# Moving the last modulation rows of a transformer block from TensorE to VectorE and GpSimd

## The chip, the core and the metric

One core of one Trainium2 chip runs the whole kernel. The metric is the device time of one execution in microseconds (us). Its engines work side by side, each through its own queue of instructions in order: TensorE (PE; its weight loads are listed as PEld), VectorE (DVE), ScalarE (ACT), GpSimd (POOL) and SyncE (SP, which here only issues DMAs).

## The reference

Input x is 2048 rows (tokens) of 1024 numbers in bf16. A condition vector c gives six modulation rows of 1024 numbers each; the block is a linear attention and a SwiGLU MLP, each behind a modulated layernorm:

```python
mod = (_silu(c) @ w_mod).reshape(c.shape[0], 6, 1, -1)
sa, ca, ga, sb, cb, gb = (mod[:, i] for i in range(6))
h = _layernorm(x) * (1 + ca) + sa
x = x + ga * linear_attention(h, wqkv, wo)     # 32 heads of 32, phi(t) = elu-like, denominator per token
h = _layernorm(x) * (1 + cb) + sb
x = x + gb * ((silu(h @ w_gate) * (h @ w_up)) @ w_down)    # hidden width 3584
```

Each row is a product of one vector of 1024 numbers with a 1024x1024 slice of w_mod (2 MB in bf16). This case is about three of them: ga (index 2), sb (3) and cb (4).

## The kernel before

**Stages.** A prologue computes silu(c), the rows sa and ca (on TensorE, loads `wme`), the layernorm of the first 512 tokens and the first K groups. Then the tokens go by in four chunks of 512 (`sc` 0 to 3). For each chunk TensorE computes K (`k_phase`, 8 groups), the previous chunk's K^T V product (`kv_phase`), and V (`v_phase`, 8 groups); a group is 8 matmuls of 128x128 by 128x512 into one accumulator. Chunk 0 also does its Q groups. After the chunks come the remaining Q groups, mixed with the folding of wo (`fold_wo`), then the attention output of chunk 0 (`wo_tile`, four tiles of 128 tokens), and then per chunk the MLP (`gate_up`, `down`), with the next chunk's `wo_tile`s inside `down`.

**Evacuation.** A K or Q group's accumulator is emptied by `phi_to`: an exp on ScalarE (L289), then two VectorE instructions (L290, L292), the last of which frees the accumulator. A V group is emptied by a ScalarE copy (L327). The accumulators of these groups (`acc_a`) rotate over four PSUM banks.

**The layernorm of the next chunk.** While chunk `sc` runs, `ln1(sc+1)` works on the next: for each of four tiles of 128 tokens, VectorE takes the BN statistics (L218, L219, `veps` L210), GpSimd raises to the power -1/2 (`rstd`, L212) and forms `nmr` (L226), ScalarE normalises to `xn` (L228), and SyncE issues a DMA that transposes `xn` into `hT` (L256). When all four have landed, VectorE scales and shifts `hT` block by block (`modulate_all`, L231, 8 instructions). The next chunk's first K group reads that `hT`. The same steps, for the second layernorm, follow each `wo_tile` (L607 to L617).

**The rows ga, sb, cb before.** `mod_load` brings 1 MB blocks of w_mod (`wml`) over SyncE's queue: two for ga in chunk 1, four for sb and cb in chunk 2. TensorE contracts them with silu(c), which was copied 32 times over columns (`sc32`), in the middle of the K phase of chunks 2 (`ga_rows`) and 3 (`mod_rows`), 32 matmuls each. ScalarE copies the result out, and GpSimd issues small DMAs that write it to DRAM and read it back: ga broadcast over the 128 partitions, sb and cb as columns (`mcol`). `ga_bc` multiplies the weights wo (L553). The row gb is done differently already: VectorE multiplies the 1024-wide row blocks with silu(c), one number per partition (`gb_sum`, L366 and L368), adding eight of them in `gb_acc`, and GpSimd sums over the 128 partitions and broadcasts (`partition_all_reduce`, L703).

**Order.** A scheduler in the framework places the instructions on each engine; `tc.issue_after(x)` gives what follows in the text no place before instruction x, and TensorE keeps the order of the text. Big buffers (`big`, 19 of 8 KB per partition) come free when their last reader is done; x1 tiles are three, ScalarE's and VectorE's scratch `e` and `eb` three each.

Of the kernel before, what the change touches and what calls it, by code (L numbers as in the profile page):

```python
# [9 lines left out]
ALU = mybir.AluOpType  # L10
# [11 lines left out]
def kernel(  # L22
# [13 lines left out]
    nc = tc.nc  # L36
# [72 lines left out]
    def acc_b(name, shape=(NB,), dt=F32):  # L109
        return pb.tile([P] + list(shape), dt, name=name, tag="pb")  # L110
# [193 lines left out]
    def k_evac(sc, gs, accs):  # L304
        for (t, nb), acc in zip(gs, accs):
            phi_to(pks[sc][:, t, nb * NB:(nb + 1) * NB], acc[:])

    def k_phase(sc, lo, hi):
        if lo == 0:
            pks[sc] = big("pk", [STC, D])  # L310
        for g in k_groups[lo:hi]:
            accs = [acc_a()]
            k_mms(sc, [g], accs)
            k_evac(sc, [g], accs)

    def v_phase(sc):
        v = big("v", [VT + DH])
# [8 lines left out]
                                     start=(cc == 0), stop=(cc == DC - 1))  # L326
                nc.scalar.copy(out=v[:, t * D + nb * NB:t * D + (nb + 1) * NB], in_=acc[:])  # L327

    def q_phase(sc, lo=0, hi=DC):
        if lo == 0:  # L330
            pqs[sc] = big("pq", [HG, SCW])
        for qc in range(lo, hi):
            acc = acc_a()
            for cc in range(DC):
                mm(acc[:], lhsT=wq[cc // 4][:, cc % 4, qc * P:(qc + 1) * P], rhs=hTs[sc][:, cc, :],
                                 start=(cc == 0), stop=(cc == DC - 1))
            phi_to(pqs[sc][:, qc, :], acc[:])

    def v_ones(v, lo):
        head = v[:, lo:lo + DH]  # L340
# [26 lines left out]
            else:  # L367
                nc.vector.scalar_tensor_tensor(out=gb_acc[:], in0=t[:], scalar=sc, in1=gb_acc[:], op0=ALU.mult, op1=ALU.add)  # L368

    def ga_rows(blks):  # L370
        ps = acc_b("modr")
        H2 = NB // 2
        for j in range(DC):
            for g in range(4):
                mm(ps[32 * g:32 * g + 32, 0:H2], lhsT=sc32[:, j, :], rhs=blks[g // 2][:, j, (g % 2) * H2:(g % 2 + 1) * H2],
                   start=(j == 0), stop=(j == DC - 1))
        row = small.tile([P, NB], BF16, name="mrow", bufs=1)
        nc.scalar.copy(out=row[:, 0:H2], in_=ps[:, 0:H2])
        for g in range(4):
            nc.gpsimd.dma_start(out=mrow_dram[0, g:g + 1, 0:H2], in_=row[32 * g:32 * g + 1, 0:H2])  # L380
        nc.gpsimd.dma_start(out=ga_bc.rearrange("p (g n) -> p g n", g=4),
                            in_=mrow_dram[0, :, 0:H2].unsqueeze(0).to_broadcast([P, 4, H2]))

    gb_rows = []

    def mod_load(cols):
        blks = []
        for lo in cols:
            t = big("wml", [DC, NB])
            nc.sync.dma_start(out=t[:], in_=wm_v[:, :, lo:lo + NB])  # L390
            blks.append(t)
        return blks

    def mod_rows(blks):
        ps = acc_b("modr")
        for j in range(DC):
            for g in range(4):
                mm(ps[32 * g:32 * g + 32, :], lhsT=sc32[:, j, :], rhs=blks[g][:, j, :],
                                 start=(j == 0), stop=(j == DC - 1))
        row = small.tile([P, NB], BF16, name="mrow", bufs=1)  # L400
        nc.scalar.copy(out=row[:], in_=ps[:])
        return row

    mrow_dram = dram.tile([2, 4, NB], BF16, name="mrow_scratch")

    def mod_spread(k, row):
        for g in range(4):
            nc.gpsimd.dma_start(out=mrow_dram[k, g:g + 1, :], in_=row[32 * g:32 * g + 1, :])
        cols = small.tile([P, 2 * DC], BF16, name="mcol", bufs=1)
        with nc.allow_non_contiguous_dma(reason="2048 elements, once"):  # L410
            nc.gpsimd.dma_start(out=cols[:], in_=mrow_dram[1].rearrange("g (i p) -> p (g i)", p=P))
        nc.vector.tensor_copy(out=sbT[:], in_=cols[:, 0:DC])
        nc.vector.tensor_scalar_add(out=cb1T[:], in0=cols[:, DC:2 * DC], scalar1=1.0)

    def modulate_all(hT, scaleT, biasT):
        for cc in range(DC):
# [21 lines left out]
    def den_spread(sc):  # L438
        rb = rbs.pop(sc)
        for q in range(STC):  # L440
            nc.gpsimd.dma_start(out=rden_dram[sc, :, q * P:(q + 1) * P], in_=rb[32 * q:32 * q + 32, :])
        rbc = big("rbc", [HG, SCW])
        rv = rden_dram[sc].rearrange("(h g) t -> h (g t)", h=HPC)
        for h in range(HPC):
            nc.gpsimd.dma_start(out=rbc[h * DH:(h + 1) * DH].rearrange("p g t -> p (g t)"),
                                in_=rv[h].unsqueeze(0).to_broadcast([DH, HG * SCW]))
        rbcs[sc] = rbc

    def den_apply(sc):
        pq, rbc = pqs[sc], rbcs.pop(sc)  # L450
# [6 lines left out]
    def keep_warm(acc, n):  # L457
        for _ in range(n):
            mm(acc[:], lhsT=sel[:, 0, :], rhs=sel[:], start=True, stop=True)

    gs = k_groups[0:6]
    accs = [acc_a() if i < 4 else acc_b("acc") for i in range(6)]
    spare = accs[5]
    keep_warm(spare, 9)
    hT = hTs[0] = big("hT", [DC, SCW])
    pks[0] = big("pk", [STC, D])
    H = 3 * P
    with in_order(nc.vector, nc.scalar, nc.gpsimd):
# [36 lines left out]
        k_mms(0, gs7, accs7, 0, A)  # L505
        for cc in range(A, DC):
            modulate(hT, cc, ca1T, saT)
        k_mms(0, gs + gs7, accs + accs7, A, DC)
        gs8, accs8 = k_groups[7:8], [acc_b("acc")]
        k_mms(0, gs8, accs8)  # L510
        k_evac(0, gs, accs)
        k_evac(0, gs7, accs7)
        k_evac(0, gs8, accs8)
    with tc.issue_after(last_on[nc.gpsimd.engine]):
        build_masks()
        nc.gpsimd.tensor_copy(out=scf[:], in_=scT[:])

    for sc in range(NSC):
# [39 lines left out]
    nc.vector.tensor_tensor(out=Zden[:], in0=kv_acc[:, :, DH:DH + 1].to_broadcast([P, HG, DH]),  # L558
# [141 lines left out]

    def gb_last():
        gb_sum(5, DC)
        nc.gpsimd.partition_all_reduce(gb_bc[:], gb_acc[:], P, bass_isa.ReduceOp.add)  # L703
# [45 lines left out]
```

## Time and profile before

| | |
|---|---|
| time, median of 3 runs | 836.31 us (836.17 to 836.62) |
| the profiled execution: its own time | 836.56 us |
| its span in the trace | 834.7 us |
| instructions | 11272 |
| DMA | 129.07 MB |

The profile is one profiled execution. Times in it are counted from the start of the span. "Busy" is the time in which an engine had an instruction at work; a group of instructions is named by line, engine, operation and what it writes and reads. The chain that ended last is followed back from the last instruction, at each step to what released it. A DMA issue has two times, that of the issue on its queue and that from issue to landing. A line of an order or a timeline may hold several like instructions ("x8"). TensorE's granted clock in that execution was 1.00 in every stage looked at.

### The profile page before, as it was taken

The numbers are of one execution on the slowest core, as the hardware profiler recorded it, in microseconds if no ns is written. First come the engines' busy times: TensorE is split into PE (matmuls) and PEld (weight loads), VectorE is DVE, ScalarE is ACT, GpSimd is POOL, SyncE is SP. The second block draws the span as 40 slices with busy tenths as digits, with TensorE's granted clock in tenths as the row PEclk, the third lists the DMA queues.
The fourth block names the chain that finished last, engine by engine and source line by source line (L and its number), as shares of the span: only waits on it lengthen the run. The fifth ranks groups of instructions, "written<-read, shape, count | busy, mean of one in ns | idle before, by whom it ended". The sixth has DMA issues, their size and how long they took to land.

```text
span 834.7 us, 11272 instructions
## 1 busy us (share of the span) xinstructions
PE 828.2 (99%) x4641; PEld 378.6 (45%) x4641; DVE 317.6 (38%) x606; ACT 168.6 (20%) x253; POOL 67.5 (8%) x168
## 2 busy tenths in 40 slices
PE   8999999999999999999999999999999999999998
PEld 3444444444444444444444444444444444444444
DVE  5755643587344335522222244211114431111122
ACT  3455443334211111101111110111110101111000
POOL 2101201111130201100000010000001100000000
PEclk9999999999999999999999999999999999999999
DMA  9873790129998644636434183662505529710011
GB/s 325 293 202 88 227 194 1 34 61 290 359 247 265 190 151 144 185 117 219 144 114 138 44 227 95 220 221 82 171 1 155 162 69 332 239 53 1 19 58 51
DMA packets 125748, 129.07 MB, mean 155 GB/s; under 512 B 34112, under 2 KB 106304, under 8 KB 125184
## 3 DMA queue, kind: packets, MB, share of 16 engines
q1 hardware_dynamic: 121440, 114.97, 45.7%
q0 software_dynamic: 3968, 12.99, 5.4%
q8 instruction: 36, 0.59, 0.3%
q10 hardware_dynamic: 288, 0.40, 0.1%
q14 instruction: 16, 0.13, 0.1%
HBM read 108.27 MB, written 12.72 MB: 145 GB/s over the span
## 4 chain that ended last, share of the span: by engine, by line
PE 95%; DMA 3%; SPq 1%; DVE 0%; issue 0%; ACT 0%
PE acc L98 88%; PE a_ps L98 7%; DMA wv<-in_A_wqkv_dram 1%; DMA x_sb<-in_A_x_dram 1%; DMA wme<-in_w_mod_dram 1%; PE kvp L98 1%; SPq L140 0%; PE modr L98 0%; PE den L98 0%; SPq L120 0%; DVE wo L577 0%; PE wf L98 0%; SPq L137 0%; DVE pq L292 0%; ACT eb L289 0%
## 5 line engine op out<-in xcount | busy, mean ns | idle before, releaser
L98 PE MATMUL acc<-h2T,wgu 128*128 128x512 bf16 x1792 | 387.6, 379 | 0.0
L98 PEld LDWEIGHTS <-wgu 128*128 128x128 bf16 x1792 | 175.3, 98 | 211.3
L98 PE MATMUL acc<-wd,gu 128*128 128x512 bf16 (+2 forms) x924 | 196.1, 373 | 0.0
L646 DVE TENSOR_TENSOR gu<-acc,e 128x512 bf16<-128x512 f32 x112 | 77.5, 692 | 289.9 <-PE acc L98 289.9
L645 ACT ACTIVATE e<-acc 128x512 f32<-128x512 f32 x112 | 66.9, 597 | 374.8 <-PE acc L98 374.8
L98 PEld LDWEIGHTS <-gu 128*128 128x128 bf16 x924 | 89.3, 98 | 104.5
L98 PEld LDWEIGHTS <-hT 128*128 128x128 bf16 x512 | 49.6, 98 | 60.0 <-issue 1.4
L667 DVE TENSOR_TENSOR e<-acc,gb_bc 128x512 f32<-128x512 f32 (+2 forms) x33 | 22.3, 675 | 131.5 <-PE acc L98 128.6
L98 PE MATMUL a_ps<-wo,pq 128*128 128x512 bf16 x256 | 57.4, 379 | 0.0
L98 PE MATMUL acc<-wk,hT 128*128 128x512 bf16 x256 | 57.1, 379 | 0.0
L98 PE MATMUL acc<-hT,wq 128*128 128x512 bf16 x256 | 56.8, 379 | 0.0
L98 PE MATMUL acc<-wv,hT 128*128 128x512 bf16 x256 | 56.1, 379 | 0.3 <-DMA wv<-in_A_wqkv_dram 0.3
L289 ACT ACTIVATE eb<-acc 128x512 bf16<-128x512 f32 x64 | 37.8, 596 | 74.1 <-PE acc L98 71.0
L228 ACT ACTIVATE xn<-x,nmr,rstd 128x1024 bf16<-128x1024 f32 x16 | 19.8, 1240 | 126.2 <-POOL nmr L226 126.2
L614 POOL DMA_DIRECT2D x_scratch<-x x16 | 9.9, 616 | 377.3 <-DVE x L607 377.3
L98 PEld LDWEIGHTS <-pq 128*128 128x128 bf16 x256 | 25.1, 98 | 30.2
L98 PEld LDWEIGHTS <-wq 128*128 128x128 bf16 x256 | 24.6, 98 | 29.8 <-issue 0.9
L290 DVE TENSOR_SCALAR eb<-eb 128x512 bf16<-128x512 bf16 x64 | 18.5, 294 | 49.4 <-ACT eb L289 49.3
L607 DVE TENSOR_TENSOR x<-a_ps,x_sb 128x512 f32<-128x512 f32 x32 | 22.1, 691 | 7.8 <-PE a_ps L98 7.7
L212 POOL TENSOR_TENSOR rstd<-veps,neg_half 128x1 f32<-128x1 f32 x32 | 17.9, 560 | 80.9 <-DVE veps L210 70.8
L327 ACT CAST v<-acc 128x512 bf16<-128x512 f32 x32 | 18.2, 582 | 23.2 <-PE acc L98 23.2
L670 DVE TENSOR_TENSOR ob<-e,x1r 128x512 bf16<-128x512 f32 (+2 forms) x33 | 22.3, 676 | 1.0
(82 smaller groups left out, 274.6 us busy)
## 6 DMA issues: line engine op xcount, KB each, us to landing
wgu<-in_B_w_gate_dram SPq DMA_DIRECT2D x28, 1024.0 KB, 7.3
wgu<-in_B_w_up_dram SPq DMA_DIRECT2D x28, 1024.0 KB, 8.8
x_sb<-in_A_x_dram SPq DMA_DIRECT2D x32, 256.0 KB, 7.2
x_scratch<-x POOLq DMA_DIRECT2D x16, 512.0 KB, 3.1
x1r<-x_scratch SPq DMA_DIRECT2D x31, 256.0 KB, 2.8
wd<-in_B_w_down_dram SPq DMA_DIRECT2D x7, 1024.0 KB, 7.3
wml<-in_w_mod_dram SPq DMA_DIRECT2D x6, 1024.0 KB, 9.0
rbc<-rden_scratch POOLq DMA_DIRECT2D x16, 256.0 KB, 9.3
```

What stands on the lines that cost most here:

```text
L98: return tc.keep_in_program_order(nc.tensor.matmul(out, lhsT=lhsT, rhs=rhs, start=start, stop=stop))
L212: nc.gpsimd.tensor_tensor(out=rstd[:, 0:n], in0=veps[:, 0:n], in1=neg_half[:].to_broadcast([P, n]), op=ALU.pow)
L228: nc.scalar.activation(out=dst, in_=src, func=ACT.Identity, bias=nmr[:], scale=rstd[:, 0:1])
L289: nc.scalar.activation(out=e[:], in_=acc, func=ACT.Exp)
L290: nc.vector.tensor_scalar(out=e[:], in0=e[:], scalar1=1.0, scalar2=PHI_EPS, op0=ALU.min, op1=ALU.add)
L327: nc.scalar.copy(out=v[:, t * D + nb * NB:t * D + (nb + 1) * NB], in_=acc[:])
L607: nc.vector.tensor_tensor(out=x1[:, ns], in0=a_ps[:], in1=x_t[:, ns], op=ALU.add)
L614: nc.gpsimd.dma_start(out=x1_dram[st * P:(st + 1) * P, :], in_=x1[:])
L645: nc.scalar.activation(out=sg[:], in_=ps[0][:], func=ACT.Silu)
L646: gm = nc.vector.tensor_tensor(out=guT[sc][f // GPT][:, f % GPT, :], in0=ps[1][:], in1=sg[:], op=ALU.mult)
L667: nc.vector.tensor_tensor(out=yt, in0=y_ps, in1=gb_bc[:, ns], op=ALU.mult)
L670: nc.vector.tensor_tensor(out=ob, in0=yt, in1=x1r, op=ALU.add)
```

## The change

For ga, sb and cb, the contraction goes the way that gb's goes already, in halves of 512 columns. `mod_begin(q)` takes an x1 tile as accumulator and loads two 1 MB blocks; `mod_step(n)` issues the next n of the 48 VectorE instructions (16 per row), each multiplying a 128x512 block by one number per partition and adding it. Their numbers per place are written out: two after each of Q groups 3 and 4 of chunk 0, `K_STEPS` of them one by one in the K phase of chunks 1 to 3 (4, 6, 8), `V_STEPS` in the V phase (6, 6, 12), two in Q group 0 of chunk 1. GpSimd sums over partitions (`mod_total`): ga in chunk 2 straight into `ga_bc`, sb in chunk 3, cb behind `den_spread(0)`; sb and cb go through DRAM in one row DMA each and come back as columns. The loads of row 2, 3 and 4 are moved to chunk 0, 1 and 2. wo x ga moves from the end of chunk 2 to the V phase of chunk 3, the copy of sb and cb into their places to behind Q group 7 of chunk 2. In the prologue, zeros matmuls that keep TensorE busy are partly issued as fp32 with half the columns of bf16's number: 4 + 1 for 9, and 3 for 6.

```diff
@@ k_phase
             k_mms(sc, [g], accs)
             k_evac(sc, [g], accs)
+            mod_step(int(k_groups.index(g) < K_STEPS[sc]))
@@
-    def q_phase(sc, lo=0, hi=DC):
+    def q_phase(sc, lo=0, hi=DC, steps=0):
...
             phi_to(pqs[sc][:, qc, :], acc[:])
+            mod_step(steps)
@@
-    def ga_rows(blks):
...
-    def mod_load(cols):
...
-    def mod_rows(blks):
...
-    def mod_spread(k, row):
...
+    mrow_dram = dram.tile([2, D], BF16, name="mrow_scratch")
+    mod_steps = []
+
+    def mod_begin(q):
+        acc = x1p.tile([P, D], F32, name="x1")
+        for half in range(2):
             t = big("wml", [DC, NB])
+            nc.sync.dma_start(out=t[:], in_=wm_v[:, :, q * D + half * NB:q * D + (half + 1) * NB])
+            mod_steps.extend((acc[:, half * NB:(half + 1) * NB], t, j) for j in range(DC))
+        return acc
+
+    def mod_step(n):
+        if n == 0:
+            return
+        with tc.issue_after(last_phi[0].ins):
+            for _ in range(n):
+                acc, t, j = mod_steps.pop(0)
+                if j == 0:
+                    nc.vector.tensor_scalar(out=acc, in0=t[:, 0, :], scalar1=scf[:, 0:1], scalar2=None, op0=ALU.mult)
+                else:
+                    nc.vector.scalar_tensor_tensor(out=acc, in0=t[:, j, :], scalar=scf[:, j:j + 1], in1=acc,
+                                                   op0=ALU.mult, op1=ALU.add)
+
+    K_STEPS = [0, 4, 6, 8]
+    V_STEPS = [0, 6, 6, 12]
+
+    def mod_total(dst, acc):
+        nc.gpsimd.partition_all_reduce(dst, acc[:], P, bass_isa.ReduceOp.add)
+
+    def mod_row(k, acc):
+        row_t = ep.tile([P, NB], F32, name="e")
+        row = row_t[:].bitcast(BF16)
+        mod_total(row, acc)
+        nc.gpsimd.dma_start(out=mrow_dram[k:k + 1, :], in_=row[0:1, :])
+
+    def mod_cols():
         cols = small.tile([P, 2 * DC], BF16, name="mcol", bufs=1)
...
+            nc.gpsimd.dma_start(out=cols[:], in_=mrow_dram[:].rearrange("k (i p) -> p (k i)", p=P))
+        return cols
@@
+    def keep_warm_f32(acc, n):
+        zeros = sel[:].rearrange("p h n -> p (h n)").bitcast(F32)
+        for _ in range(n):
+            mm(acc[:, 0:zeros.shape[1]], lhsT=zeros[:, 0:P], rhs=zeros, start=True, stop=True)
@@
-    keep_warm(spare, 9)
+    keep_warm_f32(spare, 4)
+    keep_warm(spare, 1)
@@
-        keep_warm(spare, 6)
+        keep_warm_f32(spare, 3)
@@ the loop over chunks
             k_phase(sc, 2, 4)
             if sc == 2:
-                ga_rows(blks)
-            if sc == 3:
-                mod_spread(1, mod_rows(blks))
+                mod_total(ga_bc, rows[2])
             k_phase(sc, 4, 8)
-            if sc == 1:
-                blks = mod_load([2 * D, 2 * D + NB])
-            if sc == 2:
-                blks = mod_load([3 * D, 3 * D + NB, 4 * D, 4 * D + NB])
+        if sc == 0:
+            rows[2] = mod_begin(2)
         v_phase(sc)
...
         if sc == 0:
-            q_phase(0, 0, 6)
+            q_phase(0, 0, 3)
+            q_phase(0, 3, 5, 2)
+            q_phase(0, 5, 6)
+        elif sc + 1 < NSC:
+            rows[sc + 2] = mod_begin(sc + 2)
+        else:
+            mod_row(0, rows[3])
+        if sc + 1 == NSC:
+            with tc.issue_after(last_phi[0].ins):
+                for cc in range(DC):
+                    w = wo[cc // 4][:, cc % 4, :]
+                    nc.vector.tensor_tensor(out=w, in0=w, in1=ga_bc, op=ALU.mult)
+        mod_step(V_STEPS[sc])
...
-            for cc in range(DC):
-                w = wo[cc // 4][:, cc % 4, :]
-                nc.vector.tensor_tensor(out=w, in0=w, in1=ga_bc, op=ALU.mult)
-
-    q_phase(1, 0, 2)
+
+    q_phase(1, 0, 1, 2)
+    q_phase(1, 1, 2)
@@
-    den_spread(0)
+    spread = den_spread(0)
+    with tc.issue_after(spread.ins):
+        mod_row(1, rows[4])
+        cols = mod_cols()
@@ behind q_phase(2, 6, 8)
+    with tc.issue_after(last_phi[0].ins):
+        nc.vector.tensor_copy(out=sbT[:], in_=cols[:, 0:DC])
+        nc.vector.tensor_scalar_add(out=cb1T[:], in0=cols[:, DC:2 * DC], scalar1=1.0)
```

On the built program's queues the change stands so, as far as the prediction speaks of it. GpSimd: after the rstd and nmr of chunk 1 comes an instruction that changes its loaded code, then the sum for ga, a change back, and only then the four rstd and nmr of `ln1(3)`; another change and the sum for sb in chunk 3; the sum for cb behind the DMAs of `den_spread(0)`, and the change back behind the first DMA of `wo_tile(0)`. SyncE: the 1 MB `wml` loads of rows 3 and 4 stand between the transposes of `hT` for chunks 2 and 3, the second half of each directly ahead of the fourth transpose. ScalarE: in chunk 2 each of the four normalisations stands ahead of a V copy, the first ahead of the first.

More of the change, by code (lines that the diff above doesn't have):

```diff
@@ L368, in gb_sum @@
                 nc.vector.scalar_tensor_tensor(out=gb_acc[:], in0=t[:], scalar=sc, in1=gb_acc[:], op0=ALU.mult, op1=ALU.add)
-    def ga_rows(blks):
[L371 to L382, printed above, removed]
@@ L384 @@
-    gb_rows = []
-    def mod_load(cols):
-        blks = []
-        for lo in cols:
-            t = big("wml", [DC, NB])
-            nc.sync.dma_start(out=t[:], in_=wm_v[:, :, lo:lo + NB])
-            blks.append(t)
-        return blks
-    def mod_rows(blks):
[L395 to L402, printed above, removed]
@@ L404 @@
-    mrow_dram = dram.tile([2, 4, NB], BF16, name="mrow_scratch")
-    def mod_spread(k, row):
-        for g in range(4):
-            nc.gpsimd.dma_start(out=mrow_dram[k, g:g + 1, :], in_=row[32 * g:32 * g + 1, :])
+    gb_rows = []
+    mrow_dram = dram.tile([2, D], BF16, name="mrow_scratch")
[3 more added lines that the diff above has]
+        for half in range(2):
+            t = big("wml", [DC, NB])
+            nc.sync.dma_start(out=t[:], in_=wm_v[:, :, q * D + half * NB:q * D + (half + 1) * NB])
+            mod_steps.extend((acc[:, half * NB:(half + 1) * NB], t, j) for j in range(DC))
+        return acc
@@ L409, in mod_spread @@
+    K_STEPS = [0, 4, 6, 8]
[8 more added lines that the diff above has]
+    def mod_cols():
         cols = small.tile([P, 2 * DC], BF16, name="mcol", bufs=1)
         with nc.allow_non_contiguous_dma(reason="2048 elements, once"):
-            nc.gpsimd.dma_start(out=cols[:], in_=mrow_dram[1].rearrange("g (i p) -> p (g i)", p=P))
@@ L412, in mod_spread @@
-        nc.vector.tensor_copy(out=sbT[:], in_=cols[:, 0:DC])
-        nc.vector.tensor_scalar_add(out=cb1T[:], in0=cols[:, DC:2 * DC], scalar1=1.0)
+            nc.gpsimd.dma_start(out=cols[:], in_=mrow_dram[:].rearrange("k (i p) -> p (k i)", p=P))
+        return cols
     def modulate_all(hT, scaleT, biasT):
@@ L444, in den_spread @@
         for h in range(HPC):
-            nc.gpsimd.dma_start(out=rbc[h * DH:(h + 1) * DH].rearrange("p g t -> p (g t)"),
-                                in_=rv[h].unsqueeze(0).to_broadcast([DH, HG * SCW]))
+            last = nc.gpsimd.dma_start(out=rbc[h * DH:(h + 1) * DH].rearrange("p g t -> p (g t)"),
+                                       in_=rv[h].unsqueeze(0).to_broadcast([DH, HG * SCW]))
         rbcs[sc] = rbc
+        return last
     def den_apply(sc):
@@ L516 @@
         nc.gpsimd.tensor_copy(out=scf[:], in_=scT[:])
+    rows = {}
     for sc in range(NSC):
@@ L702, in gb_last @@
         gb_sum(5, DC)
-        nc.gpsimd.partition_all_reduce(gb_bc[:], gb_acc[:], P, bass_isa.ReduceOp.add)
+        mod_total(gb_bc[:], gb_acc)
     gb_acc = x1p.tile([P, D], F32, name="x1")
```

## The prediction

> **What bounds the kernel now.** I read the engine shares first, then the chain that ended last in order of time (start us, us, what).
>
> ```profile
> PE 828.2 (99%) x4641; PEld 378.6 (45%) x4641; DVE 317.6 (38%) x606; ACT 168.6 (20%) x253; POOL 67.5 (8%) x168
> ```
> ```profile
> 20.90 10.64 DMA wv<-in_A_wqkv_dram
> ...
> 91.99 3.56 PE acc L98 x16
> 95.55 0.99 PE modr L98 x32
> 96.54 24.28 PE acc L98 x112
> ...
> 125.53 1.84 PE modr L98 x32
> ```
>
> TensorE sets the end: up to 31.5 us the chain runs through loads, then it is TensorE nearly without a gap. The two `modr` pieces, 0.99 and 1.84 us, are the contractions that the change takes off TensorE. Eight matmuls of one accumulator take 1.73 us (96.54 to 120.82 is 14 of them). So what matters is whether a chunk's `hT` is ready when its first K group wants it. That is read from the rows that scale `hT` on VectorE:
>
> ```profile
> 84.39 2.68 DVE L231 TENSOR_SCALAR hT<-hT,sca 128x512 bf16<-128x512 bf16 x8 [6.52 <-DMA hT<-xn]
> ...
> 111.69 2.67 DVE L231 TENSOR_SCALAR hT<-hT,sca 128x512 bf16<-128x512 bf16 x8 [5.38 <-DMA hT<-xn]
> ```
>
> Both wait for the last transpose by DMA. Chunk 1's V phase ends at 87.3 (63.11 + 14 x 1.73), chunk 2's at 117.3 (96.54 + 12 x 1.73). The scaled `hT` begins 2.9 us before the first and 5.6 us before the second: that is all the slack there is.
>
> **What GpSimd's sum over partitions costs.** The kernel has one already, for gb, on an idle stretch. The timeline of GpSimd:
>
> ```profile
> 269.75 6.13 POOL L703 PARTITION_ALL_REDUCE gb_bc<-x  x1 [23.39 <-DVE x L368]
> ...
> 316.94 0.58 POOL L614 DMA_DIRECT2D x_scratch<-x  x1 [39.48 <-DVE x L607]
> 325.11 0.59 POOL L212 TENSOR_TENSOR rstd<-veps,neg_half 128x1 f32<-128x1 f32 x1 [7.58 <-DVE x L607]
> ```
>
> VectorE's `veps` for that rstd was done at 317.80, yet the power began at 325.11. Between them lies only an instruction that changes GpSimd's loaded code:
>
> ```profile
> L212 POOLq MODIFY_POOL_CONFIG  x2: 37/37/37, 317.6 to 317.6; - x2
> ```
>
> From it to the first power 7.5 us pass. The other change, at 246.4, lay 23 us ahead of its sum and cost nothing. A transpose queued behind a 1 MB load is the second price; queue of SyncE, then issue to landing of that transpose, then of one at 479 us with no load just ahead:
>
> ```profile
> 328.86 0.79 SPq L631 DMA_DIRECT2D wgu<-in_B_w_gate_dram  x1
> 329.74 2.24 SPq L617 DMA_TRANSPOSE h2T<-xn  x1
> ```
> ```profile
> DMA to landing us min/median/max: 6.4/6.4/6.4
> ```
> ```profile
> DMA to landing us min/median/max: 3.2/3.2/3.2
> ```
>
> The load landed 6.3 us after its issue, at 335.2, the transpose at 336.1: 0.9 us after it.
>
> **What the Trainium skill says.** "GPSIMD Engine Reference", 2.1 Instruction dispatch: the first call after code is loaded pays about 6 us with no instruction to show for it; the trace agrees in kind and reads 7.5. "DMA: Bandwidth & Descriptors", Queues, rings and completion order: each DMA engine takes one issuer's descriptors in ring order; the 6.4 against 3.2 us fits. "Advanced Engine Details and Errata", GPSIMD Details: GpSimd conflicts with VectorE instructions in a two-port mode or with two SBUF inputs; no row of before shows it, as the VectorE rows inside the one sum read PSUM and keep 0.69 us. "TensorE: Matmul & The Clock Gate", What's actually happening: an idle window of about 3.4 us halves the clock; before never idles so long.
>
> **The change, part by part.**
>
> Removed: 64 `modr` matmuls, **-2.83 us** on the path. Their two ScalarE copies, eight small row DMAs, the broadcast of ga and its wait lay beside other work: 0.
>
> Added on VectorE: 3 x 16 steps on 128x512, by the 128x1024 rows of gb (1.28 and 0.75 us) and the 0.69 us two-input rows about 0.7 us each (0.5 the first of each half), some 33 us in chunks 0 to 3. Chunk 0: q groups 3 and 4 get two steps each; VectorE has 0.71 us free per group, so it falls 0.7 us late, the scaling of `hT` for chunk 1 starts at 57.3 instead of 56.65, wanted from 58.5: 0. A K group is 0.98 us of phi in 1.73 us; one step fits. Chunk 3: eight steps in K, then wo x ga (eight at 0.62, moved here from chunk 2 and early chunk 3) and eleven steps in V: 13.5 us from 18.7 to 32.2 us after the chunk's start, while the V phase ends at 28.8. What is late next is Zden, at 36.7, wanted at about 36.85: 0, at most +1.
>
> Chunk 1. The steps push the BN rows: the fourth `veps` comes at 79.4 instead of 77.7, so the fourth xn is done at 81.75 and its transpose issues at 81.8 (before: 80.69). The program puts the 1 MB load of the next `wml` just ahead of that transpose on SyncE's queue (issue about 81.2, once the third is issued). Landing: 81.2 + 6.3 + 0.9 = 88.4. The eight scalings start 0.334 us apart, so the eighth ends at 88.5 + 2.75; the first K group ends at about 91.3 instead of 89.0: **+2.3**. With a 3.6 us landing (85.4) it is 0; with the longest seen, 7.6, +3.3.
>
> Chunk 2. GpSimd's order is: code change (right after chunk 1's rstds, hidden), sum for ga, code change back, four rstd and nmr, all in order. In the time after the chunk-1 stall: first K group to 91.3, phi and steps 7 and 8 of the second block end at 95.35; sum to 101.5; change back, 7.5, to 109.0; first rstd and nmr to 109.9. ScalarE's order puts the first xn ahead of the first V copy, so V group 5 waits 0.25 us for its accumulator. The xn follow at 1.62 us, the fourth ends at 116.0. On SyncE the second `wml` half goes ahead of the fourth transpose again, at 115.8: landing 115.8 + 6.3 + 0.9 = 123.0, while V ends at 118.55. First K group of chunk 3 ends at 126.0 instead of 120.3: +5.75, with the 0.25 **+6.0**. With a 3.5 us landing it is +3.0; with 6 us for the change, 1.5 less.
>
> After: chunk 3's sum (rows 3) runs under the V phase and its DMA has 40 us: 0. The sum for rows 4 follows den_spread's eight DMAs, its code is loaded; its two row DMAs land (4.8 us for `mcol` before) by about 177, read at 196: 0. The change back stands behind the first x_scratch DMA, so wo_tile's first two rstd come 7.3 us late; the fourth x1 waits for the first xn (one of three buffers), the fourth transpose issues about 198.5 instead of 195.3 and lands by 202 to 206; the MLP begins at 208: 0, at most +1. Prologue: 4 fp32 zeros matmuls of 256 columns for 8 bf16 ones of 512, 3 for 6. Before has no fp32 matmul; [...]equal time: 0; at worst +1, as the stretch absorbs 0.48 + 0.57 + 0.31 us of waits ahead of 31.6; a gain is excluded since loads set that point.
>
> Unknown: two-port conflicts during the three sums, 0 to +1 us in chunk 2 (accumulators four deep cover 5 us of it), up to 6 in chunk 3, where only 0.15 us separate Zden from its reader; below 0 is excluded, as a conflict only delays. I take 0: no row of before shows one. A halved clock after the 5 us idle of chunk 2: 0 to +2.5, taken 0.
>
> Sum: -2.83 + 2.3 + 6.0 = **+5.5 us**. The profiled execution took 836.56 (span 834.7 and 1.86 around it), 0.25 over the median; from the median 836.31: **841.8**.
>
> **Rivals.**
> - *Only the first stall is missing* (the transpose isn't held behind its load in chunk 1): +3.2, 839.5. *Neither transpose is held*: -2.83 + 3.0 = +0.2, 836.5. For: loads landed in 6 to 12.8 us, so order in the ring isn't strict. Against: 6.4 against 3.2.
> - *Faster: the change back is hidden.* If code is loaded while the sum still runs, the first rstd starts at 101.5, before V's first copy; then xn, transposes and scaling keep their slack and -2.83 stays: 833.5. It decides if the first rstd comes within 2.5 us of the sum's end and the chunk-1 transpose within 5 us. Against: 325.11.
> - *Slower still: VectorE is held by the three sums and TensorE's clock drops*: 5.5 + 2.5 + up to 6 (the third chunk's sum delaying Zden): 847 to 855.
> - That TensorE keeps the rows is excluded: in the built program no `modr` matmul is left on TensorE.
>
> **How the numbers follow.** Both stalls 0.55 (841.8; own range 839 to 844.5), one stall 0.12 (of it 0.02 below 838), neither 0.11, faster 0.12, slower still 0.10. Within 0.2% (1.7 us, about what this measurement can tell) is 834.6 to 838.0, so: faster 0.12, same 0.11 + 0.02 = 0.13, slower 0.55 + 0.10 + 0.10 = 0.75. The range 835.5 to 848 leaves out the faster case and most of the last, 0.19 together.
>
> **What would show it.** TensorE waiting for `hT` ahead of the first K group of chunks 2 and 3 (about 1.5 and 5 us); the first chunk-2 rstd 7 us behind the sum; the landing of the fourth transposes over 6 us. No such wait and a sum followed at once by rstd would prove me wrong, as would a VectorE gap during a sum.

## The result and the profile after

The changed kernel takes **859.21 us** (median of 4 runs, 858.32 to 859.45), the kernel before 836.30 (836.17 to 836.62): ratio 1.0271, 95% interval 1.0254 to 1.0289, so 22.9 us slower where 5.5 were forecast. Times here and below are medians; one execution of the last experiment's kernel took 1777 us, for which the runs show no reason, and is outside its ratio. The profiled execution has a span of 857.6 us (before: 834.7), so the two traces show the whole difference.

The engine line of the page, and the view of what TensorE waited for (in total, times, longest):

```profile
PE 828.6 (97%) x4498; PEld 380.2 (44%) x4577; DVE 359.2 (42%) x654; ACT 167.2 (20%) x251; POOL 84.8 (10%) x164
```
```profile
PE acc L98 <- DVE hT L231: 7.9, 2, 5.8
PE acc L98 <- issue: 3.9, 7, 2.9
PE wf L98 <- DVE wo L594: 3.2, 2, 3.0
PE acc L98 <- DVE pk L292: 2.0, 4, 0.8
PE tp L101 <- DVE kvs L571: 1.9, 1, 1.9
...
PE acc L98 <- ACT v L328: 0.5, 2, 0.3
```

TensorE has fewer matmuls and is as long busy as before: part of them ran slower. Four of these lines name VectorE, and one names nothing ("issue": the engine waited for nothing that the profile shows). Of its seven times only the longest is a loss. The other six are 0.16 us each, and the piece behind each is one matmul record short (x15 for 16, x47 for 48):

```profile
167.44 1.22 PE L98 MATMUL kvp<-v,pk 128*32 128x64 bf16 x128
168.82 3.40 PE L98 MATMUL acc<-hT,wq 128*128 128x512 bf16 x15 [0.16 <-issue]
```

From 167.44 to the end of the second line are 4.78 us, as many as for the same two pieces before (151.58 to 152.73 + 3.63). To see where the lag grows, the starts of the same piece of TensorE's work are read from its timeline in both traces:

| piece of TensorE's work | before | after | lag, us |
|---|---|---|---|
| first V group of chunk 1 | 73.41 | 73.69 | 0.3 |
| first K group of chunk 2 | 87.22 | 89.74 | 2.5 |
| first K group of chunk 3 | 117.20 | 129.52 | 12.3 |
| first V group of chunk 3 | 134.22 | 149.14 | 14.9 |
| first q group behind chunk 3 | 148.03 | 163.90 | 15.9 |
| transposes of KVB (L101) | 156.20 | 174.12 | 17.9 |
| first wo_tile | 176.93 | 199.79 | 22.9 |

From there on the lag stays. TensorE's timeline, two pieces before the change and then the four longest waits after it (the bracket is the idle time ahead):

```profile
103.39 13.98 PE L98 MATMUL acc<-wv,hT 128*128 128x512 bf16 x64
117.20 3.62 PE L98 MATMUL acc<-wk,hT 128*128 128x512 bf16 x16
```
```profile
89.74 5.88 PE L98 MATMUL acc<-wk,hT 128*128 128x512 bf16 x16 [2.07 <-DVE hT L231]
...
129.52 5.09 PE L98 MATMUL acc<-wk,hT 128*128 128x512 bf16 x16 [5.80 <-DVE hT L231]
...
140.94 8.36 PE L98 MATMUL acc<-wk,hT 128*128 128x512 bf16 x38 [2.92 <-issue]
...
189.81 0.37 PE L98 MATMUL wf<-wo,kvs 32*32 32x512 bf16 x1 [2.99 <-DVE wo L594]
```

The end of a piece is modelled: before, the V phase is shown to end at 117.37, yet the next group starts at 117.20. So an interruption costs about 0.16 us more than the idle that is shown. The two waits for `hT` are those of the forecast. But the 16 matmuls behind them take 5.88 and 5.09 us, not 3.62 as before. The stages view shows why (its last three columns are the granted clock, the DMA share and GB/s):

```profile
92.00:93.00 1.00, 1.00 (x4) 0.45 (x4) 0.00 (x0) 0.25 (x1) 0.00 (x0) 0.50 0.00 0
93.00:94.00 1.00, 1.00 (x4) 0.39 (x3) 0.59 (x2) 0.35 (x1) 0.00 (x0) 0.50 0.07 16
...
130.50:131.50 1.00, 1.00 (x4) 0.36 (x3) 1.00 (x4) 0.00 (x0) 0.00 (x0) 0.50 1.11 221
```

TensorE ran at half its clock. Such stretches lie at 91.6 to 95.0, 129.1 to 132.5 and 190.5 to 194.0, each 3.41 us long and worth up to 1.71 us of work at full clock. The first begins while the group is still paced by the scaling of `hT`, the second 0.4 us before the idle ends, so these two are worth about 1.5 us each (5.09 for 3.62). Then VectorE during the three sums: GpSimd's rows, and below them VectorE's, both from the timeline:

```profile
98.10 6.13 POOL L401 PARTITION_ALL_REDUCE e<-x  x1 [16.50 <-DVE x L394]
111.63 0.59 POOL L212 TENSOR_TENSOR rstd<-veps,neg_half 128x1 f32<-128x1 f32 x1 [7.40 <-DVE veps L210]
...
149.94 6.13 POOL L401 PARTITION_ALL_REDUCE e<-x  x1 [13.95 <-DVE x L394]
...
183.79 6.07 POOL L401 PARTITION_ALL_REDUCE e<-x  x1
```
```profile
99.27 3.52 DVE L290 TENSOR_SCALAR eb<-eb 128x512 bf16<-128x512 bf16 x1 [0.96 <-ACT eb L289]
103.43 1.09 DVE L392 TENSOR_SCALAR x<-wml,scf 128x512 f32<-128x512 bf16 x1
...
110.98 0.15 DVE L210 TENSOR_SCALAR veps<-mv 128x1 f32<-128x1 f32 x1
...
150.32 4.44 DVE L392 TENSOR_SCALAR x<-wml,scf 128x512 f32<-128x512 bf16 x1
154.67 1.54 DVE L290 TENSOR_SCALAR eb<-eb 128x512 bf16<-128x512 bf16 x1
...
183.24 5.19 DVE L290 TENSOR_SCALAR eb<-eb 128x512 bf16<-128x512 bf16 x1 [0.71 <-ACT eb L289]
```

The `eb` row takes 0.29 us everywhere else. Inside a sum it ends 4.6 to 4.8 us after the sum's start (102.79, 154.76 for L392, 188.43), and in the first two sums a second TENSOR_SCALAR row ends within 0.3 us of the sum's end. As VectorE works in order, phi and with it the accumulators wait behind such a row.

### The profile page after: what moved, and what is told of

The parts are those of the page before. It is cut to its first block, busy times and chain, and to the rows that moved or that the text cites. A ratio compares the mean times of both kernels' runs of the same rounds, so it can differ in the third digit from the quotient of the medians.

```text
span 857.6 us, 11110 instructions
## 1 busy us (share of the span) xinstructions
PE 828.6 (97%) x4498; PEld 380.2 (44%) x4577; DVE 359.2 (42%) x654; ACT 167.2 (20%) x251; POOL 84.8 (10%) x164
## 4 chain that ended last, share of the span: by engine, by line
PE 87%; DVE 7%; issue 2%; DMA 2%; ACT 1%; POOL 1%; DVEq 0%; POOLq 0%; ACTq 0%
PE acc L98 80%; PE a_ps L98 6%; DVE x L394 2%; DMA hT<-xn 2%; DVE eb L290 2%; DVE stats L218 1%; DVE pk L292 1%; DVE x L392 1%; DVE wo L552 1%; POOL rstd L212 0%; ACT xn L228 0%; ACT eb L289 0%; PE kvp L98 0%; POOL nmr L226 0%; PE mod_ps L98 0%
## 5 line engine op out<-in xcount | busy, mean ns | idle before, releaser
L98 PE MATMUL acc<-wk,hT 128*128 128x512 bf16 x251 | 60.5, 394 | 11.3 <-DVE hT L231 7.9
L290 DVE TENSOR_SCALAR eb<-eb 128x512 bf16<-128x512 bf16 x64 | 27.6, 436 | 28.7 <-ACT eb L289 28.7
L394 DVE SCALAR_TENSOR_TENSOR x<-wml,scf,x 128x512 f32<-128x512 bf16 x42 | 30.4, 747 | 0.2
```

What stands on the lines that cost most here:

```text
L98: return tc.keep_in_program_order(nc.tensor.matmul(out, lhsT=lhsT, rhs=rhs, start=start, stop=stop))
L290: nc.vector.tensor_scalar(out=e[:], in0=e[:], scalar1=1.0, scalar2=PHI_EPS, op0=ALU.min, op1=ALU.add)
L394: nc.vector.scalar_tensor_tensor(out=acc, in0=t[:, j, :], scalar=scf[:, j:j + 1], in1=acc, op0=ALU.mult, op1=ALU.add)
```

## The experiments

Each run is compared with runs of the kernel before on the same chip.

**The sums left out (e3_no_sums).**

```diff
+    def mod_copy(dst, acc):
+        nc.scalar.copy(out=dst, in_=acc[:])
...
-        mod_total(row, acc)
+        mod_copy(row, acc)
...
-                mod_total(ga_bc, rows[2])
+                mod_copy(ga_bc, rows[2])
```

> The changed kernel, but the three sums over partitions are left out: a ScalarE copy of the partial sums to bf16 (128x1024) stands in their place, and every VectorE step stays. Theory A (the sums cost: VectorE held during them about 8.7 us in all, and the wait ahead of chunk 3 through GpSimd's order): the VectorE rows of 3.5 to 5.2 us go back to 0.3 and 0.5, no wait of TensorE for pk, kvs or wo remains, the first rstd of chunk 2 comes at about 104: 841 to 845. Rival (the 33 us of added VectorE steps themselves make phi and Zden late): TensorE still waits for VectorE in chunk 3 and the time stays above 850.

846.53 us, ratio 1.0119 (1.0102 to 1.0136): 12.7 below the changed kernel and 1.5 above the upper end of what was expected. The waits for `pk`, `v` and `kvs` are gone and `wo` is back to the 0.2 of before; no long VectorE row is left. What remains is 6.8 us for `hT` in two waits, 1.7 of issue and three 3.41 us stretches of half clock. So the sums, with the code changes around them, cost 12.7 us here, somewhat over half of the loss. The first rstd was expected at 104 and came at 107.47, and VectorE's rows say why:

```profile
107.17 0.15 DVE L210 TENSOR_SCALAR veps<-mv 128x1 f32<-128x1 f32 x1
```

With no sum at all the row statistics are ready only at 107.17, which is 17.2 us after the chunk's first K group; in the kernel before it is 12.6 us (99.79 after 87.2). The added steps delay them by 3.6 us of these 4.6 (in e5, below, with the first groups at full clock, `veps` comes at 103.17, 16.15 us after the first K group at 87.02); the other 1.0 goes with the half clock behind the wait for `hT`. In the changed kernel the held rows add 4 (110.98, 21.2 us after).

**Which VectorE instructions a sum holds (e4_held_ops, and the first part of e6_idle_clock).** The kernel before, with extra sums in the MLP and a row of one kind of instruction behind each:

```diff
+        nc.vector.memset(dst[:, 0:2], 0.0)          # the sum starts behind this
+        nc.gpsimd.partition_all_reduce(dst, src, P, bass_isa.ReduceOp.add)
+        for k in range(12):
+            nc.vector.tensor_scalar(...)            # or one of the other kinds
```

> The kernel before, with four extra sums over partitions (128x1024) in the last MLP chunk, each followed by twelve VectorE instructions of one kind on 128x512 bf16 in SBUF: TENSOR_SCALAR with one input, SCALAR_TENSOR_TENSOR with two inputs, TENSOR_TENSOR with two inputs, BN_STATS. Theory A (the sum locks the shared SBUF port against VectorE's two-port modes only): TENSOR_SCALAR and TENSOR_TENSOR bf16 are held by up to 4.7 us once and 1.4 us once, SCALAR_TENSOR_TENSOR and BN_STATS keep their length. Rival (every VectorE instruction that reads SBUF is held): all four kinds show rows of over 3 us. Rival (nothing is held by the sum; the long rows came from late inputs): none does.

By tile, e4's three kinds (ns: shortest/median/longest), and by line e6's two, BN_STATS and TENSOR_SCALAR from PSUM:

```profile
L716 DVE TENSOR_SCALAR e<-wd x12: 281/294/4597, 721.1 to 730.8; 128x512 bf16<-128x512 bf16 x12
L718 DVE SCALAR_TENSOR_TENSOR e<-wd,scf x12: 741/752/4905, 750.5 to 764.2; 128x512 bf16<-128x512 bf16 x12
L720 DVE TENSOR_TENSOR e<-wd x12: 414/424/4640, 778.6 to 788.4; 128x512 bf16<-128x512 bf16 x12
```
```profile
L726 DVE BATCH_NORM_STATS2 eb<-wd x10: 682/694/695, 396.7 to 404.1; 128x6 f32<-128x512 bf16 x10
```
```profile
L728 DVE TENSOR_SCALAR eb<-junk x10: 680/691/691, 438.3 to 445.8; 128x512 bf16<-128x512 f32 x10
```

TENSOR_SCALAR on SBUF and both kinds with two SBUF inputs have one row that is 4.2 to 4.3 us too long; BN_STATS with one SBUF input and the same TENSOR_SCALAR reading PSUM keep their length. The expectation for SCALAR_TENSOR_TENSOR was wrong: it is held as well, so the modulation steps themselves are. A second hold, to the sum's end, is seen for TENSOR_SCALAR alone (a row of 1.56 us from 726.10, the sum ends at 727.51); the rows with two SBUF inputs keep 0.42 and 0.75 us from their release (783.71 and 756.17) to the end of their sums (785.01 and 757.20). e4's fourth stretch did not run (there are only seven blocks in a chunk), and e4's time of 845.54, one execution with a load 5.4 us late in its prologue, is not read; neither is e6's. The Trainium skill, "SBUF — State Buffer", Who interferes with whom, names just this set (two-port modes always, two SBUF inputs against a GpSimd instruction that reads SBUF) and says that the loser waits for the whole instruction; the traces agree on the set, but not on the length: the sum of 6.1 to 6.5 us lets go 4.6 to 5.5 us after its start.

**The row loads behind the transposes (e1_loads_late).**

```diff
-            rows[sc + 2] = mod_begin(sc + 2)
+            with tc.issue_after(last_tr[0].ins):    # the fourth transpose of the chunk
+                rows[sc + 2] = mod_begin(sc + 2)
```

> The changed kernel, but the two 1 MB row loads of chunks 1 and 2 are issued behind the fourth transpose of their chunk on SyncE's queue. Theory A (the transpose is held by the load ahead of it): both fourth transposes land in about 3.6 us instead of 6.4 and 6.9; the 2.07 us wait ahead of the first K group of chunk 2 goes, and with it 0.7 us of pacing and 1.7 us of halved clock behind it; the 5.8 us wait ahead of chunk 3 falls to about 2.5. In all 8 to 11 us less than the changed kernel: 848 to 851. Rival (the fourth transpose is late because VectorE, with its added steps, finishes the row statistics late): the landing stays above 6 us or the wait stays, and the time is above 856.

849.09 us, ratio 1.0154 (1.0139 to 1.0169): 10.1 less than the changed kernel, as theory A said. Issue to landing of the transposes, in the changed kernel and in this one:

```profile
DMA to landing us min/median/max: 3.1/3.6/6.9
```
```profile
DMA to landing us min/median/max: 3.0/3.1/3.5
```

Chunk 2's first K group starts at 87.52 with no wait; the wait ahead of chunk 3 falls from 5.8 to 2.0 us.

**The ga sum behind the rstds (e2_sum_late).**

```diff
-            if sc == 2:
-                mod_total(ga_bc, rows[2])
...
+            with tc.issue_after(last_nmr[0].ins):   # the fourth nmr of chunk 2
+                mod_total(ga_bc, rows[2])
```

> The changed kernel, but the sum over partitions for ga stands behind the four rstd and nmr of chunk 2 on GpSimd instead of ahead of them. Theory A (the sum and the code change back, 6.1 and 7.4 us, delay the fourth xn): the first rstd comes at about 104 instead of 111.6, the 5.8 us wait ahead of chunk 3 falls below 2 us; the sum now runs at about 116 to 123 and its hold on VectorE falls on the scaling of hT instead of on phi, so some 1 to 4 us stay: 851 to 855. If the code change costs nothing, the first rstd moves by 6 us at most and the wait stays near 5 us: 857 to 860.

856.24 us, ratio 1.0238 (1.0222 to 1.0253): 3 us gained, between the two ranges that were expected; the wait ahead of chunk 3 is still 5.9 us. The first rstd comes at 107.78, 0.14 us after `veps` is done (107.49 and 0.15 long), hence VectorE sets it here. The sum now runs from 122.17 to 128.43, and what it holds is the scaling of `hT` itself:

```profile
124.90 5.29 DVE L231 TENSOR_SCALAR hT<-hT,sca 128x512 bf16<-128x512 bf16 x8 [8.68 <-DMA hT<-xn]
```

Eight rows take 5.29 us instead of 2.68, with TensorE waiting. The clock view of this run shows five stretches of half clock against three (three of them in a row from 124.4), up to 3.4 us more, so part of what the move gained was lost again there.

**Both causes away, and a version that keeps the result (e5_late_no_sums, b1_sums_on_pe).** e5 is e1 and e3 together. b1 is e1 with the sums on TensorE:

```diff
+            mm(ps[:], lhsT=ones[:], rhs=row[:, half * NB:(half + 1) * NB], start=True, stop=True)   # ga, two halves
...
+            mm(ps[:, i:i + 1], lhsT=row[:, i * P:(i + 1) * P], rhs=ones[:, 0:1], start=True, stop=True)   # columns, 8 per row
```

> The changed kernel with the row loads behind the fourth transposes and the three sums over partitions left out (a ScalarE copy of the partial sums stands in their place; every VectorE step stays). Theory A (the loss is the held transposes, the held VectorE with the code change, and what follows from both: clock and late instructions): of the loads-late kernel's 849.1 us go the waits for wo, pk and hT (3.1, 2.2, 2.0), two stretches of halved clock (1.5 each) and about 1 us of issue: 836 to 839, no halved clock in chunks 0 to 3. Rival (the added VectorE steps alone make chunk 3 late): waits of TensorE for kvs or pk of over 2 us remain, 842 or more.

> The steps stay on VectorE, the row loads go behind the fourth transposes, and the sums over partitions are done by TensorE on the partial sums cast to bf16 by ScalarE: two matmuls with a matrix of ones for ga (broadcast at once), and eight matmuls of one column for each of the other two rows, which land as columns. Theory A: as the run without sums, plus 2 x 0.22 and 16 x about 0.07 us on TensorE, 837 to 840; against the kernel before it keeps 2.83 - 1.5 = 1.3 us of the gain at best, 835. Rival (VectorE's steps make chunk 3 late whatever does the sums): 842 or more.

840.80 us, ratio 1.0049 (1.0035 to 1.0063), and 841.02, ratio 1.0053 (1.0039 to 1.0067): 18 of 22.9 us are back, but both lie above their expectation. The rival is not met either: no wait for `kvs` or `pk` is left. The two profiled executions have no half clock in the chunks, but they are not typical (e5's took 838.53, 2.3 below the median): three of e5's four and three of b1's five executions have a mean granted clock of 0.997 or 0.998, as one or so stretch of half clock would give (1.71 of 840 us is 0.002). TensorE's waits in b1, with its prologue's left out:

```profile
PE acc L98 <- issue: 3.2, 2, 2.8
PE acc L98 <- DVE hT L231: 1.5, 1, 1.5
```

The added VectorE steps alone cost no wait in chunk 3's q groups. The rest in these profiles is chunk 2's late row statistics and the issue gap, and in the other executions, it seems, the half clock that such an idle can bring.

**The clock (e6_idle_clock).** A one-matmul wait of chosen length behind each block of two MLP chunks:

```diff
+        nc.vector.memset(z[:], 0.0)
+        for _ in range(n):                          # n = 0, 3, 6, 9, 12, 16, 20
+            nc.vector.tensor_scalar(out=z[:], in0=z[:], ...)
+        mm(junk[:, 0:P], lhsT=z[:, 0:P], rhs=z[:, 0:P], start=True, stop=True)
```

> The kernel before with additions in the MLP: in its second chunk two extra sums over partitions, followed by ten BN_STATS on SBUF and ten TENSOR_SCALAR that read PSUM; in its third and fourth chunk, after each block, a small matmul that waits for a chain of 0 to 20 VectorE instructions, so that TensorE idles about 1.5 to 6.5 us, each length twice. Theory A (a clock gate on a fixed grid of about 3.41 us: a grid cell with more than about 1.4 us of idle halves the clock for the next cell): idles above about 2.8 us are always followed by a stretch of PEclk 0.5 of about 3.4 us, those of 1.5 to 2.8 only where they fall within one cell. Rival (only an idle of a whole 3.4 us halves it): nothing below 3.4 us is followed by it. For the held kinds: BN_STATS and PSUM sources keep 0.69 and about 0.7 us during the sum; if every SBUF read is held, BN_STATS shows a row above 3 us.

Idles of 1.13, 2.11 and 2.47 us were followed by no half-clock stretch; 3.10 by one of 3.41 us, both times; 4.08 by one; 5.07 by one or two; 6.38 by two; 7.69 by two or three. TensorE's timeline shows one of the 3.10:

```profile
575.83 0.29 PE L98 MATMUL junk<-eb 128*128 128x128 bf16 x1 [3.10 <-DVE eb L712]
```

If the starts of these stretches are laid on a grid of 3.41 us, the most idle time in a cell at full clock that was not followed by half clock is 1.8 us here, and the least that was followed 2.35: the 1.4 us of the expectation is too low. An idle need not fill a cell: that rival is out. The traces give no sharper limit. Behind the prologue, every cell of the other runs with 2.0 us or more was followed (e8, below: 2.0 and 2.07), but 1.84 (e8) and 1.94 (e2) were too, and 1.96 in the changed kernel (122.3 to 125.7) was not. The grid also fits that the 2.07 us wait (with the gaps of the paced matmuls behind it) slowed TensorE while the 2.92 us issue gap, which lies across two cells with 1.3 and 1.6 us in them, did not.

**The issue gap (e8_wo_early, e7_traffic, b2_early_loads, b3_spread).** The DMA view lists packets of the kind "instruction". In the changed kernel one moves at 138.27, while the engines are full, and TensorE goes on 2.7 us later, at 140.94:

```profile
q8 instruction: 1, 0.02, 34.0%
```

e8 is the changed kernel with one edit, so that TensorE's instructions stay what they were (chunk 2's two row loads move too, behind its fourth transpose):

```diff
             kv_phase(sc - 1)
+            if sc == 2:
+                wo = [...]                          # taken and loaded here, not after the chunk
             k_phase(sc, 2, 4)
```

> The changed kernel with one edit: the two wo tiles are taken and loaded behind the second K group of chunk 2 instead of after the chunk; TensorE's, VectorE's and ScalarE's instructions and their order stay the same. (With wo ahead of them, the two row loads of chunk 2 also go behind the fourth transpose.) Theory A (the 2.9 us issue gap in chunk 3 comes from instructions fetched beside the wo loads): the gap in chunk 3 goes or falls below 1 us, a smaller one may open in chunk 2 beside the loads there; the wait for hT ahead of chunk 3 falls from 5.8 to about 2.5; 851 to 854. Rival (the gap is a property of that place in the stream): a gap of 2 to 3 us stays in chunk 3's K phase, 855 or more.

850.81 us, ratio 1.0176 (1.0162 to 1.0190). The wait ahead of chunk 3 is 0.3 us, less than expected. The gap in chunk 3 is 0.94 us, and beside the loads, now in chunk 2, another has opened, larger than expected, and wide enough for half clock behind it:

```profile
101.09 9.69 PE L98 MATMUL acc<-wk,hT 128*128 128x512 bf16 x37 [2.35 <-issue]
```

e7 adds to the kernel before four 1 MB loads that nobody reads, behind the wo loads.

> The kernel before plus four loads of 1 MB each from DRAM to DRAM that nothing waits for, issued on SyncE's queue behind the wo loads, at about 114 us; no engine's other work changes. Theory A (instructions of TensorE are fetched by the same DMA engines and arrive late while these are full): TensorE shows an idle of 1 to 3 us put down to issue in chunk 3's K phase, near 122 to 130, that the kernel before does not have, and the time rises by about as much, 837.5 to 839.5. Rival (the gap in the changed kernel comes from its own instruction order or waits): no such gap, 836.3.

837.49 us, ratio 1.0014 (1.0007 to 1.0021). Here theory A's gap did not come. The instruction packet of that place did move later, from 122.60 to 125.45, but TensorE went on working. The loss is elsewhere: the row for `mcol` arrived late behind the loads, VectorE waited for it, and TensorE 1.5 us for `pk`. Full DMA engines alone don't make a gap; that TensorE must also be near the end of what it has is likely, and not shown.

b2 is b1 with the row loads issued behind the second K group of chunks 1 and 2, wo behind that of chunk 2, and four VectorE steps moved behind the statistics (`K_STEPS = [0, 4, 2, 8]`, `V_STEPS = [0, 6, 10, 12]`); b3 puts wo behind the fourth transpose and the ga matmuls into chunk 3.

> The kernel with the sums on TensorE, but the row loads and the eight wo loads are issued early in chunks 1 and 2 (behind the second K group, when the DMA engines are idle) instead of behind the transposes, and four steps move from chunk 2's K phase to its V phase, behind the row statistics. Theory A (what is left of the loss is TensorE's own instructions arriving late behind 4 MB of loads, 2.2 to 2.8 us, and the late fourth transpose of chunk 2, 1.3 to 1.5 us): no wait named issue and no wait for hT in chunk 3, 835 to 837, within 0.2% of the kernel before. Rival (TensorE's issue gap doesn't depend on the loads): the gap stays at about 128 us and the time is 838 or more.

> The kernel with early loads and the sums on TensorE, with two edits: wo is loaded behind the fourth transpose of chunk 2, so that only 2 MB of rows go out early in chunk 2; and the two ones matmuls for ga with their ScalarE copies move into chunk 3's K phase, off the ScalarE queue of chunk 2's V phase. Theory A (TensorE's instructions come late when a block of them is fetched while the DMA engines are full): the 1.9 us idle put down to issue at 95 us shrinks below 0.7, the 0.8 us wait for v goes, and unless a gap opens in chunk 3 beside the wo loads the time is 835 to 836.5. Rival (the gap belongs to that place in the instruction stream whatever is loaded): it stays at 1.9, 837 or more.

837.54 us, ratio 1.0016 (1.0010 to 1.0023), and 837.26, ratio 1.0015 (1.0007 to 1.0023), both just above what was expected. In both the wait for `hT` is gone, so the moved steps brought the statistics in time. The gap moved with the loads: b2 has none in chunk 3 but one of 1.87 us in chunk 2 (and a wait of 0.8 us for `v`); b3 has 0.83 and 1.91. The changed kernel and the nine made from it have 14 such gaps of over 0.3 us, all begun within 4 us of the start of a burst of 128 small matmuls (`kvp`), and in each the instruction packet starts 2.5 to 3.0 us ahead of TensorE's next matmul. Each of these kernels has four bursts. Where the DMA engines were over half busy in the 2 us ahead of the packet next to the burst, 14 of 16 bursts have a gap; where they moved nothing, none of 24. So the gap needs busy DMA engines, and e8 moves it by moving loads alone. That the late packet is what TensorE waits for is read from these times; no run delays the packet alone, and the kernel before and e7 have two bursts each beside full engines without a gap.

**Loads placed between those packets (b4_between_fetches).** b3 with all four row loads in chunk 1 and wo behind chunk 2's second K group:

```diff
-            if sc < 3:
-                rows[sc + 2] = mod_begin(sc + 2)
+            if sc == 1:
+                rows[3], rows[4] = mod_begin(3), mod_begin(4)
+            if sc == 2:
+                wo = [...]
```

> The kernel with the sums on TensorE, loads placed between the places where TensorE's instruction blocks were seen to arrive (about 92 to 94 and 121 to 125 us): all four row loads of 1 MB go out in chunk 1 behind its second K group, the first wo tile at about 87, the second when row 2's steps are done at about 95, nothing near chunk 3's K phase. Theory A: the two issue gaps of 0.8 and 1.9 us of the kernel with spread loads shrink, chunk 3's to zero and chunk 2's below 0.8; what is left of the gain is 2.83 - 1.5 us of TensorE work: 834.5 to 836. If the gap in chunk 2 stays (the loads at 87 to 92 are still under way at 93) 836 to 837. Rival (the four row loads now hold chunk 1's transposes): a wait for hT ahead of chunk 2's first K group, 838 or more.

835.82 us against 836.48 for the kernel before, ratio 0.9992 (0.9984 to 1.0001). What TensorE still waits for in chunks 0 to 3:

```profile
PE acc L98 <- issue: 1.1, 6, 0.3
PE acc L98 <- DVE hT L231: 0.4, 1, 0.4
```

Five of the six "issue" times are again 0.16 us with a matmul record missing behind them; the sixth, 0.34, is a gap in chunk 1 beside the loads. All of the loss is gone, and the gain that is left can't be told from none.

## Why the prediction was wrong

The forecast failed in three terms that it put at nothing: VectorE held by the sums (measured 6.9 us), half clock (4.7) and TensorE's late instructions (2.9). The two stalls that it did price came out close to the forecast.

| step | forecast, us | measured, us |
|---|---|---|
| `modr` off TensorE | -2.83 | gone, as forecast |
| chunk 1: transpose behind its load, paced first group | +2.3 | 2.07 wait, 0.7 paced |
| chunk 2: wait ahead of chunk 3, and V behind xn on ScalarE | +6.0 | 5.8 and 0.5 |
| VectorE held by the sums (pk, kvs, wo) | 0, bounds 0 to 7 | 2.0 + 1.9 + 3.0 = 6.9 |
| half clock after idles | 0, bounds 0 to 2.5 | 1.5 + 1.5 + 1.7 = 4.7 |
| issue gap | not seen | 2.9 |
| eleven new interruptions, about 0.16 each beyond the idle shown | not seen | 1.8 |
| sum | +5.5 | 22.5 of 22.9 |

- **The two stalls: right in size, one of them for half the wrong reason.** Landings of 6.4 and 6.9 us behind the loads are as forecast, and e1 shows the cause. In chunk 2, however, the forecast let GpSimd's order set the first rstd (sum, then 7.5 us for the change back). The change did take 7.4 (104.23 to 111.63), but `veps` was not ready before 111.13 either. The step that failed is that the VectorE steps in chunk 2's K phase cost nothing: they, the half clock and the held rows pushed the statistics by 8.6 us (3.6, 1.0 and 4.0 by e3 and e5), and the change back was hidden but for half a microsecond. e2 took it away, and the wait stayed at 5.9. That the size came out right is in part luck: the fourth transpose was forecast to land at 123.0 and the V phase to end at 118.6; they came at 129.0 and 123.7, both over 5 us later.
- **VectorE held by the sums: the term mis-sized at 0.** It was listed, bounded at 0 to 7, and set to 0 because no row of before showed it. The rows inside the one sum of before all read PSUM, and those are just the kind that is not held (e6); they said nothing on `eb`, which works in SBUF. The measured 6.9 is at the upper end. It came in all three places: the first sum delays V of chunk 2, the second V of chunk 3 and Zden, the third the wo copies of the fold (3.0 us), a place where the forecast had looked for no such hold.
- **The clock: the size per event was known, the number not.** The forecast allowed one half-clock stretch, behind the longest idle. The Trainium skill, "TensorE: Matmul & The Clock Gate", What's actually happening, asks for a whole idle window of about 3.4 us; the runs show 3.41 us cells, of which about 2 idle are enough. So three idles, of 2.07, 5.8 and 2.99 us, each brought one.
- **Issue: not seen at all.** The kernel before has loads beside the same stretches and no gap. The eight wo loads, issued from 103.6 to 113.1 us before, now stand behind the late fourth transpose on SyncE's queue, are issued from 124.5 to 129.2 and run into chunk 3's K phase, where the one gap of 2.9 us stands. The forecast followed SyncE's queue only as far as the transpose and never asked what the entries behind it would meet.
- **Right:** chunk 0 and the prologue at no cost (0.3 us of lag at 73 us), no stage later than the first wo_tile hurt, although its first rstds came 7 us late, and the sign. Of the rivals, "slower still" named two of the three missing causes, at a chance of 0.10. Its end of 855 does not follow from its terms, though: 836.3 + 5.5 + 2.5 + 6 is 850.3.

## What to carry to other kernels

A sum on GpSimd is not free because GpSimd is idle: in its 6 us it can hold each VectorE instruction of the kinds above for over 4, and one such instruction on the path of the accumulators stops the lot. Price a stall on TensorE with what follows it: half clock for the next cell where about 2 us of the idle fall into one, and every load that is queued behind the late one and now meets another stage. And a bound that rests on "no row shows it" should be read from rows of the same kind, or the middle of the bound taken.

## What the runs showed of the hardware

- A 128x1024 sum over partitions of 6.1 us holds VectorE's TENSOR_SCALAR on SBUF and its instructions with two SBUF inputs to 4.6 to 5.5 us after its start. TENSOR_SCALAR is then held again, to the sum's end, the others are not (0.42 and 0.75 us, as without a sum). BN_STATS and PSUM sources go through at 0.69 us.
- TensorE's clock falls to half for 3.41 us at a time when the cell of that length ahead of it has about 2 us of idle in it, up to 1.7 us lost each time. From 2.0 us on it always did (behind the prologue), below 1.8 it did only where matmuls were paced as well (1.6 in the changed kernel); between, 1.84 and 1.94 did and 1.96 did not.
- TensorE can run out of instructions: behind 14 of 16 bursts of small matmuls beside busy DMA engines, and none of 24 beside idle ones, it stood still for 0.3 to 2.9 us, and went on 2.5 to 3.0 us after a packet of the kind "instruction".
